# A per-slot list of weight-conversion steps for the first batch of a fused threshold-attention and GELU kernel

## The chip, the cores and the metric

The kernel runs on one core of a Trainium2 chip. The metric is the device time of one execution in microseconds (us). Three executions of the kernel before took 1337.2, 1337.45 and 1339.41 us; their median, 1337.45 us, is the time before. One further execution was recorded by the profiler and is the source of every profile line below.

## What is computed

```python
def _attn_ref(q, k, v, tau):                      # q, k, v: (8, 8, 576, 64) float32
    scores = (1 / np.sqrt(64)) * np.matmul(q, k.transpose(0, 1, 3, 2))
    thresh = np.max(scores, axis=-1, keepdims=True) - tau
    scores = np.where(scores >= thresh, scores, -1e9)
    attn = np.exp(scores - np.max(scores, axis=-1, keepdims=True))
    attn = attn / (np.sum(attn, axis=-1, keepdims=True) + 1e-09)
    return np.matmul(attn, v)
# heads joined: x is (4608, 512); w_in (512, 2048) and w_out (2048, 512) arrive as float64
h = x @ w_in
g = 0.5 * h * (1.0 + erf(h / sqrt(2)))
out = (g @ w_out).astype(np.float32)
```

So there are 64 heads of attention (8 batches of 8 heads), in which only scores close to the row's maximum count, and after it a two-layer network with an exact GELU over 4608 tokens. The change touches the way the two weight matrices become float32.

## The kernel before, in words

**Pairs and slots.** Two heads of one batch form a pair `p` (0 to 31, four per batch). The queries of a pair are worked on in five chunks `i`: four chunks of 128 queries for each of the two heads (two units of work), and a fifth chunk, `i == NC`, that holds the last 64 queries of both heads (one unit). One (pair, chunk) is a slot `n`. The loop at L1086 runs over the slots, and each engine is given its instructions in the order in which this loop writes them. The first batch is slots 0 to 19: slots 0 to 7 are chunks 0 and 1 of pairs 0, 1, 2, 3; then come chunks 2, 3, 4 of pair 0 (slots 8 to 10), of pair 1 (11 to 13), of pair 2 (14 to 16) and of pair 3 (17 to 19). Slots 10, 13, 16 and 19 have one unit, the others two.

**One slot of the first batch**, in program order:

- `scores` (L408): TensorE computes q·k into `sc`, of which two buffers exist in PSUM. A buffer comes free when `softmax_tail` of the slot before has read it.
- `softmax_head`: for each unit VectorE takes the row maximum `nmx` (L420), GpSimd the threshold `thr` (L423), and ScalarE the exponential `p` (L425). `add_low_bits` (L224) puts the outstanding additions of converted weights on GpSimd; the newest one is put ahead of the first `thr`.
- `turn_qk_early` (L324 to L341) in slots 0, 2 and 4: TensorE transposes q and k of the next pair, and ScalarE copies them out.
- `gelus` (L603): ScalarE copies finished pieces `hT` of the first layer out of PSUM.
- `weigh_v`, `weigh_half` and `divide_early` (L544, L568, L463; ScalarE copies at L554, L570, L465; GpSimd products at L471): the weighted values x^T of earlier chunks. In slots 12, 15 and 18 this is the long form, with 320 columns.
- `fill` (L636, L651): TensorE works on the two-layer network of finished tokens, from slot 10 on.
- `turn_p_early` (L354, ScalarE copies at L361, L365, L370, L374): transposes the exponentials of the slot before.
- `softmax_tail` (L441): VectorE sets exponentials below the threshold to zero and sums the rest.
- loads of later pairs: `load(HP)` in slot 13 and `load(HP + 1)` in slot 17 put 16 DMAs each on SP's queue.
- `convert` (L1160), the last large part of a slot.

TensorE's transposes, scores' partners `xT`, `tr`, and the network's `hT` share four PSUM buffers (tag "mm"), each freed by the copy that reads it.

**Conversion.** The weights come as 32 pieces of 128 x 512 float64 numbers, 512 KB each (16 of `w_in`, 16 of `w_out`). `load_piece` (L183) puts a load on SP's queue; eight are loaded at the start, and each finished piece starts the load of the next. A step of the generator `conversions` (L186) handles one piece: ScalarE makes a scaled copy of the high words (L202, `power`) and a copy of the low words (L203, into the weights), one piece ahead; VectorE shifts and masks (L210) and joins sign and magnitude (L211) in the older piece; GpSimd adds the two parts (L224) in the next slot. `fill` takes a matmul only when the pieces that it reads are converted.

**How many steps in which slot.** `convert(ns)` adds `ns` to a debt and takes steps until the debt is gone; each finished step pays 1060. Slot 0 adds nothing, slots 1 and 2 add 1200 each, later ones 1900, and slot 19 takes what is left. This gives two steps in most slots and one in some. `yield None` holds the last two pieces back for slot 19.

Of the kernel before, what the change touches and what calls it, by code (L numbers as in the profile page):

```python
# [18 lines left out]
def kernel(  # L19
# [141 lines left out]
    def load_piece(eng=nc.sync):  # L161
        k = loaded[0]
        if k == len(pieces):
            return
        staged = k % 2 and k < len(pieces) - LATER
        if wide and not staged and not x_free:
            return
        dst, src = pieces[k]
        loaded[0] += 1
        if not wide:  # L170
            nc.sync.dma_start(dst, src)
            converted[0] += 1
            load_piece()
            return
        slot = []
        if staged:

            half, at = divmod(k // 2 % 4, 2)
            raw = pd[half].bitcast(U32)[:, at * 2 * PIECE:(at + 1) * 2 * PIECE]
        else:  # L180
            slot = [x_slot()]
            raw = x_rows(slot[0]).bitcast(U32)
        eng.dma_start(raw, src.bitcast(U32))  # L183
        raws.append((dst, raw, slot))

    def conversions():  # L186

        vec = nc.vector
        ahead = []
        done = 0
        while raws or ahead:
            if raws:
                dst, raw, slot = raws.pop(0)
                lo, hi = (raw.rearrange("p (f w) -> p f w", w=2)[:, :, i] for i in range(2))  # L200
                power = gp.tile([P, PIECE], U32, tag="g", name="power")
                nc.scalar.activation(power.bitcast(FP32), hi.bitcast(FP32), AF.Copy, bias=0.0, scale=2.0 ** -112)  # L202
                nc.scalar.activation(dst.bitcast(U32), lo, AF.Copy, bias=0.0, scale=2.0 ** -29)  # L203
                ahead.append((dst, hi, power, slot))
                yield 0
            if len(ahead) == LATER and done == len(pieces) - LATER:
                yield None
            if len(ahead) == 2 or not raws:
                dst, hi, power, slot = ahead.pop(0)
                vec.tensor_scalar(power, power, 3, 0x7FFFFFF8, op0=ALU.logical_shift_left, op1=ALU.bitwise_and)  # L210
                vec.scalar_tensor_tensor(power, hi, 0x80000000, power, op0=ALU.bitwise_and, op1=ALU.bitwise_or)  # L211
                x_free.extend(slot)
                sums_due.append((dst.bitcast(U32), power))
                load_piece()
                done += 1
                yield 1060

    sums_due = []

    def add_low_bits(newest=False):  # L220

        for _ in range(min(1, len(sums_due)) if newest else len(sums_due)):
            dst, power = sums_due.pop(-1 if newest else 0)
            nc.gpsimd.tensor_tensor(dst, power, dst, op=ALU.add)  # L224
            converted[0] += 1
# [3 lines left out]
    def convert(ns, least=0):  # L229

        if conv["steps"] is None:
            conv["steps"] = conversions()
        conv["debt"] += ns
        while conv["debt"] > 0 or least > 0:
            took = next(conv["steps"], None)
            if took is None:
                return
            conv["debt"] -= took
            least -= took
# [5 lines left out]
    def load(p):  # L245
        for _ in load_steps(p):
            pass
# [151 lines left out]
    def scores(p, i):  # L399
        s = st[p]  # L400
        n = 1 if i == NC else 2
        sc = s["sc", i] = [ps.tile([P, 2, 512], FP32, tag="sc", name="sc", bufs=2) for _ in range(n)]
        for h in range(2):
            for e in range(n):
                rows = slice(0, P) if i == NC else slice(e * D, (e + 1) * D)
                lhsT = s["q_tail"] if i == NC else s["qT"][rows, i * P:(i + 1) * P]
                at = h * HALF + (TAIL if p < EARLY and e == 0 else 0)
                nc.tensor.matmul(  # L408
                    sc[e][:, h, 0:HALF], lhsT=lhsT, rhs=s["kT"][rows, at:at + HALF], start=True, stop=True)
# [37 lines left out]
    def invert(p, i):  # L447

        den = st[p]["sum", i]
        nc.vector.reciprocal(den, den)  # L450
# [608 lines left out]
    BATCH = HP * SLOTS  # L1059
# [16 lines left out]
    PARTS = 1.3, 1.3, 0.2, 1.3, 0.9  # L1076

    HALVED = (2, 3)
    BUSY = {1: 2, 6: 2, 8: 2, BATCH: 4}

    tokens = 0
# [4 lines left out]
    for n in range(len(slots) + WEIGH + 1):  # L1086
        p, i = slots[n] if n < len(slots) else divmod(n, SLOTS)
        early = p < EARLY
        last = slots[n - 1] if 0 < n <= len(slots) else None
        if p < NP:  # L1090
            scores(p, i)
            softmax_head(p, i)
            add_low_bits()
            if last and last[0] < EARLY:
                invert(*last)
            if p < HP - 1 and i == 0:
                turn_qk_early(p + 1)
        elif n == len(slots):
            early_end.close()
            weights_first()  # L1100
        gelus(0)
        if n == BATCH:
            gelus_held()
        table()
        for args in due:
            if len(args) == 2:
                weigh_half(*args)
                if args[1]:
                    divide_early(args[0], 0, TOK)
                continue  # L1110
            weigh_v(*args)
            divide_early(*args)
        due = []
        if p > EARLY and i == WEIGH:
            for lo, hi in (0, WIDE), (WIDE, S):
                weigh_v(p - 1, lo, hi)
            if p == NP:
                divide(p - 1)
        owed += (goal(n) - goal(n - 1)) * BLK_NS * (PARTS[i] if not early and p < NP else 1.0)
        if early:  # L1120
            fill(owed, tokens)
            owed = 0.0
            table()
        if last and last[0] < EARLY and last[1] < NC:
            turn_p_early(*last)
        if p < NP:
            softmax_tail(p, i)
        if p < NP and not early:
            turn_p(p, i)
        if p < NP and not early:  # L1130
            if i == 2:
                regroup(p, 1)
            if i > 2:
                regroup(p, i)
            if i == NC:
                divisors(p)
        if last and last[0] < EARLY and last[1] == NC:
            turn_p_early(*last)
        if p < 2 and i == 0:
            for _ in range(2):  # L1140
                load_piece()
            load_v_early(p + 2)
        if p == 1 and i == NC:
            load(HP)
        if n == BATCH - 3:
            load(HP + 1)
        if n == BATCH:
            for t in pd_tail + [turned_p[:, e, h, :, :] for e in range(2) for h in range(2)]:
                nc.gpsimd.memset(t[:, NB:4 * KR, :], 0.0)
        if EARLY < p < NP and i == DIVIDE:  # L1150
            divide(p - 1)
        if p >= HP and i == 1 and p + 2 < NP:
            loads = load_steps(p + 2)
        if p >= HP:
            next(loads, None)
        if p >= HP and i == 1 and p + 1 < NP or p == HP - 1 and i == 2:
            scale_q(p + 1)
        if p >= HP - 1 and i == 2 and p + 1 < NP:
            turn_qk(p + 1)
        convert(0 if n == 0 else 1200 if n < 3 else 1900 if n < BATCH - 1 else 1e9)  # L1160
        if not early:
            lag[0] = 2 if p < NP else 0
            if n != BATCH:
                share = 0.4 if n == BATCH + 1 else 1.0
                fill(owed * share, tokens)
                owed *= 1.0 - share
        if n in BUSY:
            keep_busy(BUSY[n])
        if last and last[0] < EARLY:
            if last[1] < 2 and last[0] in HALVED:  # L1170
                due.append((last[0], last[1]))
            elif last[1] == 1:
                due.append((last[0], 0, TOK))
            if last[1] == NC:
                due.append((last[0], TOK, S))
        if n == START - 1:
            tokens = TOK
        elif n == BATCH + 1:
            tokens = S
        elif p > EARLY and i == DIVIDE and p % HP == 0 or p == NP and i == WEIGH:  # L1180
            tokens = p // HP * S
            leaving += [n for n in AWAY if n in x_blk and (n + 1) * TOK <= tokens]
        elif leaving and i < 2:
            put_away(leaving.pop(0))
# [35 lines left out]
```

## Time and profile before

| | before |
|---|---|
| median of three executions | 1337.45 us |
| the profiled execution, its own time | 1338.74 us |
| span of its instructions on the core | 1336.9 us |
| TensorE busy in the span | 1318.9 us (99%) |
| VectorE, ScalarE, GpSimd busy | 1038.9, 605.4, 633.6 us |
| conversions: ScalarE L202, L203 | 32 + 32 instructions, first at 16.88 us, last at 124.05 us |
| conversions: VectorE L210, L211 | 32 + 32 instructions, first at 17.61 us, last at 128.19 us |
| conversions: GpSimd L224 | 32 instructions of 1270 ns |

The table mixes three kinds of number. The span runs from the first to the last instruction of the profiled execution; its own time is 1.84 us longer, for what lies around the instructions. Busy times are sums over the whole span, and say little of one stage: the first batch ends some 130 us after the start, and only there do conversions run. The profile can be asked for each engine's instructions in order of time, with the idle time before each and the engine that ended it; for the busy time of every engine in a stretch; and for the chain of work that ended last. Times in it count from the start of the span. The slots can be read off VectorE's row maxima (L420), whose first one in a slot marks it:

| slot | first row maximum, us | steps of conversion in the slot |
|---|---|---|
| 1 | 13.69 | 2 |
| 2 | 19.82 | 1 |
| 3 | 25.47 | 2 |
| 4 | 32.58 | 1 |
| 5 | 37.41 | 2 |
| 6 | 44.36 | 2 |
| 7 | 49.79 | 2 |
| 8 | 55.75 | 2 |
| 9 | 61.17 | 1 |
| 10 | 66.08 | 2 |
| 11 | 71.50 | 2 |
| 12 | 76.93 | 2 |
| 13 | 86.31 | 1 |
| 14 | 90.55 | 2 |
| 15 | 96.68 | 2 |
| 16 | 105.15 | 2 |
| 17 | 110.15 | 2 |
| 18 | 117.94 | 0 |
| 19 | 124.29 | 2 |
| 20 | 129.03 | |

The third column counts VectorE's pairs L210, L211 between one slot's `p` (L441) and the next slot's maximum.

### The profile page before, as it was taken

To read this page: it belongs to the slowest core of one execution; us is meant where nothing else is said; L and a number is where in the kernel's file an instruction comes from. 1 tells how busy PE (TensorE), PEld (TensorE's weight loads), DVE (VectorE), ACT (ScalarE), POOL (GpSimd) and SP (SyncE) were. 2 spreads that over 40 slices of the span, in tenths; PEclk is the share of its full clock that TensorE was granted. 3 is DMA by queue.
4 is the path that set the end of the run, shared out by engine and by line. 5 is a ranking of instruction groups with operands and counts; after the bars stand their busy time and mean duration, and the time that the engine had idled before them with its cause. 6 is when DMAs were issued, how large, how long until landed. Compare 5 with 4: busy or idle time off the path is not lost.

```text
span 1336.9 us, 19969 instructions
## 1 busy us (share of the span) xinstructions
PE 1318.9 (99%) x6362; PEld 893.4 (67%) x6362; DVE 1038.9 (78%) x2005; ACT 605.4 (45%) x1029; POOL 633.6 (47%) x1061
## 2 busy tenths in 40 slices
PE   8899999999999999999999999999999999999998
PEld 6677466466466466457556557568787787877877
DVE  6877777788888888888888888783857698386775
ACT  7987457268367358338438438322211113211120
POOL 3655454555555555545546551245264503635530
PEclk9999999999999999999999999999999999999999
DMA  8553566776776786786787775400000130000003
GB/s 258 196 150 62 124 151 141 167 183 153 175 188 153 179 201 153 180 209 155 165 219 164 164 187 124 106 9 1 1 0 1 40 101 18 0 1 0 1 0 79
DMA packets 209784, 152.42 MB, mean 114 GB/s; under 512 B 113360, under 2 KB 193088, under 8 KB 209680
## 3 DMA queue, kind: packets, MB, share of 16 engines
q1 hardware_dynamic: 192256, 127.21, 40.1%
q0 software_dynamic: 16992, 23.64, 6.7%
q8 instruction: 52, 0.85, 0.3%
q14 instruction: 52, 0.43, 0.1%
q10 hardware_dynamic: 432, 0.30, 0.1%
HBM read 55.97 MB, written 12.52 MB: 51 GB/s over the span
## 4 chain that ended last, share of the span: by engine, by line
PE 92%; DVE 2%; ACT 2%; DMA 2%; SPq 1%; issue 1%; POOL 0%; ACTq 0%; DVEq 0%
PE bank L824 34%; PE o_ps L651 17%; PE hT L636 16%; PE sc L408 13%; PE xT L544 11%; ACT p L425 1%; DVE nmx L420 1%; DMA q<-in_q_dram 1%; PE tr L354 1%; DMA x<-xall 1%; DVE power L211 1%; DMA turned_p<-in_moe_w_in_dram 0%; ACT pT L361 0%; DVE p L441 0%; DVE power L210 0%
## 5 line engine op out<-in xcount | busy, mean ns | idle before, releaser
L425 ACT ACTIVATE p<-sc,nmx 128x576 f32<-128x576 f32 x288 | 201.8, 737 | 272.7 <-DVE nmx L420 272.2
L441 DVE SCALAR_TENSOR_TENSOR p<-sc,thr,p 128x576 f32<-128x576 f32 x288 | 225.3, 816 | 74.8 <-ACT p L425 65.1
L423 POOL TENSOR_SCALAR thr<-nmx,tau_eff 128x1 f32<-128x1 f32 x288 | 83.9, 293 | 341.9 <-DVE nmx L420 337.6
L636 PE MATMUL hT<-xall,w_in 128*128 128x256 f32 x1024 | 242.0, 386 | 0.5 <-ACT g L603 0.5
L420 DVE TENSOR_REDUCE nmx<-sc 128x1 f32<-128x576 f32 x288 | 205.4, 750 | 44.5 <-PE sc L408 43.1
L651 PE MATMUL o_ps<-w_out,g 128*128 128x512 f32 x512 | 236.8, 603 | 0.0
L636 PEld LDWEIGHTS hT<-xall,w_in 128*128 128x128 f32 x1024 | 189.3, 190 | 50.8 <-issue 23.0
L706 DVE TENSOR_TENSOR c<-c,bank 128x320 f32<-128x320 f32 x304 | 146.7, 487 | 34.2 <-PE bank L824 21.0
L706 DVE TENSOR_TENSOR o<-o,bank 128x256 f32<-128x256 f32 x240 | 99.8, 419 | 93.7 <-PE bank L824 88.7
L651 PEld LDWEIGHTS o_ps<-w_out,g 128*128 128x128 f32 x512 | 93.1, 190 | 109.2 <-issue 106.8
L408 PE MATMUL sc<-kT,qT 64*128 64x288 f32 x960 | 159.9, 431 | 2.1 <-DVE p L441 1.6
L544 PE MATMUL xT<-pT,v 128*64 128x320 f32 (+1 forms) x1240 | 159.9, 411 | 0.6 <-DVE pT L365 0.5
L505 DVE STREAM_TRANSPOSE turned_p<-p 128x1152 f32<-128x1152 f32 x112 | 154.4, 1378 | 3.9
L408 PEld LDWEIGHTS sc<-kT,qT 64*128 64x128 f32 x960 | 91.0, 186 | 75.8 <-issue 60.1
L544 PEld LDWEIGHTS xT<-pT,v 128*64 128x64 f32 x1240 | 86.7, 137 | 71.9 <-issue 11.3
L824 PE MATMUL bank<-w_out,c 128*128 128x256 f32 x480 | 120.2, 381 | 0.5 <-DVE o L706 0.5
L267 POOL DMA_DIRECT2D v<-in_v_dram x208 | 110.8, 536 | 4.3 <-issue 2.1
L824 PEld LDWEIGHTS bank<-w_out,c 128*128 128x128 f32 x480 | 89.9, 190 | 18.8 <-DVE o L706 3.0
L877 ACT ACTIVATE c<-c 128x320 f32<-128x320 f32 (+1 forms) x80 | 46.9, 623 | 114.6 <-DVE c L706 114.5
L824 PE MATMUL bank<-t_out,c 128*128 128x256 f32 x320 | 82.8, 381 | 0.0
L706 POOL TENSOR_TENSOR c<-c,g 128x320 f32<-128x320 f32 (+1 forms) x40 | 50.5, 1271 | 67.5 <-DVE c L706 67.5
L824 PE MATMUL bank<-t_out,g 128*128 128x256 f32 x320 | 82.1, 379 | 0.0
(180 smaller groups left out, 1757.7 us busy)
## 6 DMA issues: line engine op xcount, KB each, us to landing
pT<-turned_p SPq DMA_DIRECT2D x448, 160.0 KB, 3.5
pT<-pd_tail SPq DMA_DIRECT2D x112, 80.0 KB, 2.7
q<-in_q_dram POOLq DMA_DIRECT2D x104, 72.0 KB, 3.7
k<-in_k_dram POOLq DMA_DIRECT2D x104, 72.0 KB, 3.1
inv<-turned SPq DMA_DIRECT2D x54, 128.0 KB, 4.0
v<-in_v_dram POOLq DMA_DIRECT2D x156, 40.0 KB, 3.1
out_dram<-o SPq DMA_DIRECT2D x40, 128.0 KB, 2.3
xall<-in_moe_w_out_dram SPq DMA_DIRECT2D x9, 512.0 KB, 4.1
```

The costliest lines, as they stand in the source:

```text
L267: eng.dma_start(t[r:P:4, e, 0:n, :], rows[:, r * KR:r * KR + n, :])
L408: nc.tensor.matmul(sc[e][:, h, 0:HALF], lhsT=lhsT, rhs=s["kT"][rows, at:at + HALF], start=True, stop=True)
L420: nc.vector.tensor_reduce(nmx[:, e:e + 1], sc, axis=AXIS.XY, op=ALU.max, negate=True)
L423: nc.gpsimd.tensor_scalar(thr[:, e:e + 1], nmx[:, e:e + 1], -1.0, tau_eff, op0=ALU.mult, op1=ALU.subtract)
L425: nc.scalar.activation(w[:, e * S:(e + 1) * S].rearrange("p (h s) -> p h s", h=2), sc, AF.Exp, bias=nmx[:, e:e + 1], scale=1.0)
L441: nc.vector.scalar_tensor_tensor(row, sc[e][:, :, 0:HALF], thr[:, e:e + 1], row, op0=ALU.is_ge, op1=ALU.mult, accum_out=den[e])
L505: nc.vector.transpose(turned_p[:, :, i // 2, 0:NB, i % 2 * Q:(i % 2 + 1) * Q], w.rearrange("p (e b i) -> p e b i", e=2, i=Q))
L544: nc.tensor.matmul(to, lhsT=s["v"][:, e, c, :], rhs=rhs, start=(c == 0), stop=(c == KR - 1))
L636: nc.tensor.matmul(hT[:, j % 2, :], lhsT=w_in_sb[c][:, j * P:(j + 1) * P], rhs=x_blk[n][:, c, :], start=(c == 0), stop=(c == N_DM - 1))
L651: nc.tensor.matmul(o[:, 0:d_model], lhsT=g[j][:, m * P:(m + 1) * P], rhs=w_out_sb[j], start=(j == 0), stop=(j == N_DF - 1))
L706: eng.tensor_tensor(out, a, b, op=ALU.add)
L824: nc.tensor.matmul(to, lhsT=l, rhs=r, start=start and k == 0, stop=k == len(pairs) - 1, skip_group_check=not start)
```

## The change

The debt in nanoseconds gives way to a list `STEPS` with the number of steps for each slot from 0 to 18. A finished step now counts 1, and `convert(0, STEPS[n])` takes steps until that number is reached, or until `yield None`. Slot 19 takes the rest, as before.

```diff
@@ conversions @@
-                yield 1060
+                yield 1
...
     HALVED = (2, 3)
+    STEPS = [0, 1, 1, 1, 1, 1, 2, 1, 2, 1, 2, 2, 3, 2, 2, 3, 2, 2, 3]
...
-        convert(0 if n == 0 else 1200 if n < 3 else 1900 if n < BATCH - 1 else 1e9)
+        if n < BATCH - 1:
+            convert(0, STEPS[n])
+        else:
+            convert(1e9)
```

The built program differs from the one before in this: VectorE has one pair L210, L211 less in slots 1, 3, 5 and 7, and one more in slots 12, 13, 15 and 18. ScalarE's pairs L202, L203 follow one piece ahead of these (slot 1 has two pieces on ScalarE where it had three, slot 18 has two where it had one). TensorE's order is the same, instruction for instruction. On SP's queue six loads of pieces stand behind the 16 loads of `load(HP)`, where three stood; on GpSimd's the additions follow their pieces. The number of instructions of each kind is the same.

## The prediction

> **What bounds the kernel now.** I first read the page's totals, then the busy time of each engine in stretches of 10 us, then each engine's instructions in order of time.
>
> ```profile
> PE 1318.9 (99%) x6362; PEld 893.4 (67%) x6362; DVE 1038.9 (78%) x2005; ACT 605.4 (45%) x1029; POOL 633.6 (47%) x1061
> ```
> ```profile
> 40.00:50.00 10.00, 8.67 (x90) 6.77 (x87) 9.23 (x20) 9.64 (x20) 4.40 (x7) 1.00 0.35 116
> 90.00:100.00 10.00, 10.00 (x70) 7.22 (x67) 8.46 (x20) 8.83 (x19) 5.29 (x9) 1.00 0.64 110
> ```
>
> Over the span TensorE (PE) is busy 99%, so time can only be won where it waits. The stretches (columns: length, then PE, PEld, VectorE, ScalarE, GpSimd, clock, DMA share, GB/s) show where: from 40 to 50 us TensorE is busy 8.67 us and ScalarE 9.64; from 90 to 100 us TensorE is full. So slots 1 to 9 hang on ScalarE and VectorE, slots 13 to 16 on TensorE. ScalarE in slot 7:
>
> ```profile
> 50.57 1.41 ACT L425 ACTIVATE p<-sc,nmx 128x576 f32<-128x576 f32 x2 [0.42 <-DVE nmx L420]
> ...
> 54.53 0.73 ACT L202 ACTIVATE power<-xall 128x512 f32<-128x512 f32 x1
> 55.12 0.72 ACT L203 ACTIVATE w_in<-xall 128x512 uint32<-128x512 uint32 x1
> 56.53 1.41 ACT L425 ACTIVATE p<-sc,nmx 128x576 f32<-128x576 f32 x2 [0.69 <-DVE nmx L420]
> ```
>
> It works without a gap up to the end of the second piece, then waits 0.69 us for the next row maximum. That maximum stands on VectorE behind the second conversion:
>
> ```profile
> 53.08 0.96 DVE L210 TENSOR_SCALAR power<-power 128x512 uint32<-128x512 uint32 x1
> 54.08 0.69 DVE L211 SCALAR_TENSOR_TENSOR power<-xall,power 128x512 uint32<-128x512 uint32 x1
> 54.69 0.42 DVE L210 TENSOR_SCALAR power<-power 128x512 uint32<-128x512 uint32 x1
> 55.14 0.69 DVE L211 SCALAR_TENSOR_TENSOR power<-turned_p,power 128x512 uint32<-128x512 uint32 x1
> 55.75 1.42 DVE L420 TENSOR_REDUCE nmx<-sc 128x1 f32<-128x576 f32 x2
> ```
>
> The scores of slot 8 were due from TensorE at about 54.4 us, so one conversion would fit into that wait and the second doesn't. Slot 12, ScalarE, then TensorE:
>
> ```profile
> 83.37 1.07 ACT L361 COPY pT<-tr 128x512 f32<-128x512 f32 x2 [3.06 <-PE tr L354]
> ...
> 85.69 0.66 ACT L202 ACTIVATE power<-turned_p 128x512 f32<-128x512 f32 x1
> 86.25 0.67 ACT L203 ACTIVATE w_out<-turned_p 128x512 uint32<-128x512 uint32 x1
> 87.10 0.74 ACT L425 ACTIVATE p<-sc,nmx 128x576 f32<-128x576 f32 x1 [0.17 <-DVE nmx L420]
> 87.73 0.58 ACT L603 COPY g<-hT 128x512 f32<-128x512 f32 x1
> ```
> ```profile
> 87.74 1.60 PE L354 MATMUL tr<-ident,p 128*128 128x128 f32 x9
> ```
>
> ScalarE idles 3.06 us here, but ahead of the pT copy, which waits for TensorE; the conversions stand behind that copy. And TensorE's nine transposes take 1.60 us (elsewhere 1.15): five of them begin at 88.37, just after the copy of hT frees a PSUM buffer at 88.31. So ScalarE's lateness here is at once TensorE's.
>
> **What the Trainium skill says.** "TensorE: Matmul & The Clock Gate", section "What's actually happening": the clock falls to half after an idle window of about 3.4 us. The trace agrees:
>
> ```profile
> 21.00:22.00 1.00, 0.10 (x1) 0.00 (x0) 0.66 (x3) 1.00 (x3) 1.00 (x4) 1.00 0.53 149
> 24.00:25.00 1.00, 1.00 (x7) 0.48 (x4) 0.27 (x1) 0.98 (x3) 0.58 (x1) 0.50 0.91 299
> ```
>
> After a gap from 21.1 to 22.64 us the clock is 0.50 from about 23.6 to 27 us. The same page, "Architectural detail", says that ScalarE and VectorE run strictly in order; the two slots above show it. "SBUF — State Buffer", section "SBUF: two separate sides": VectorE and GpSimd share a port pair, and the later one waits. The L210 of 0.96 us above (median 0.424) stands beside a GpSimd L471 at 53.03 to 53.76.
>
> **The change, part by part.** Prices: a piece on ScalarE takes 1.15 us (two steps of 0.57 from start to start); a pair on VectorE 1.07 us (53.08 to 54.69 is 1.6 with the port wait, 54.69 to 55.75 is 1.06).
>
> *Removed in slots 1, 3, 5, 7* (interval from one exponential to the next, before; after).
> - Slot 1: 14.48 to 20.60, 6.12 us. VectorE's one pair ends 18.7, the maximum follows, exponential at 19.45: saves 1.15.
> - Slots 2 and 3: slot 2 is full on ScalarE (5.87 us), so it moves as a whole, and slot 3's exponential to 25.3. But TensorE's transposes of q and k don't move, so the gap that ended at 22.64 shrinks from 1.53 to about 0.4 us, and I expect no half clock. Then slot 3's scores take 1.24 us for 2.08, xT 2.5 for 3.18, and xT, from the copy of pT it needs (24.1), ends at 26.6 for 28.5. ScalarE's copies of xT, inv and pT are done 2.3 us after that, as now (28.5 to 30.79), and one piece later, at 30.0, comes the exponential of slot 4, now at 33.37: 3.35 in all, so 2.2 more than slot 1 gave (1.37 if the half clock stays: a piece and the wait of 0.2 behind it).
> - Slot 5: 5.91 us, full on ScalarE. Without a piece 4.5; VectorE's one pair (0.4 port wait) gives 4.65: saves 1.25.
> - Slot 7: 5.96. One pair with its port wait ends 1.1 sooner, and a little from GpSimd: saves 1.2.
>
> Sum: 5.8 us by slot 9; bounds 4 (half clock stays, scores late) and 6.5. Slots 4, 6, 8, 9 keep their counts and lengths.
>
> *Added in slots 12, 13, 15, 18.* In slot 12 ScalarE's third piece comes after 86.84, VectorE's third pair waits for it, GpSimd's newest addition (1.27) precedes the threshold: the exponential of slot 13 moves from 87.10 to 88.2, the copy of hT, the transposes and the scores of slot 14 with it: +1.1. Slot 13, in today's times with 1.1 added: VectorE's first pair ends at 91.1; the second waits for ScalarE's copies of pT and the L202 of its piece (91.5) and ends at 92.6; the maximum follows, and the exponential of slot 14 stands at 93.4 for 91.34, 2.0 late: +0.9. Slot 15's scores begin at 93.78, the masks of slot 14 end at 93.67, so there is no slack. In slot 15 ScalarE waits for TensorE at the copy of pT anyway (2.17 us idle), but then three pieces follow where two did; slot 17's scores wait for slot 16's mask (ended 107.71): +1.1. In slot 18 VectorE's pair lies in its 2.97 us idle time, free; with that cover gone it would cost 1.07. ScalarE's second piece pushes slot 19's exponential by 0.7, of which 0.5 reaches slot 20's maximum. Sum +3.6; bounds 1.5 (slots 12 and 15 hidden) and 4.5.
>
> *Queues.* SP: the 16 loads of slot 13 take 10.6 us to issue (86.84 to 97.46), and six pieces, not three, come behind them: in the changed kernel from about 81.5 + 10.6 = 92 us. At the 110 to 186 GB/s moved between 90 and 110 us a piece of 512 KB lands every 2.8 to 4.8 us (an estimate). The first two are on ScalarE at about 105, the next two at 112: hidden, with 1 to 8 us spare. GpSimd: a third addition follows the thresholds of slots 13 and 16 and delays only a product for tokens used later: nothing, and at most 1.27 us each if that product were awaited.
>
> Net: -5.8 + 3.6 = -2.2 us. From slot 20 on both kernels are the same and TensorE is full, so the shift stays. Span 1336.9 - 2.2 = 1334.7; with the 1.84 us around it 1336.5 against 1338.74. That execution lay 1.3 above the median, so the median goes from 1337.45 to 1335.2.
>
> **Rivals.**
> 1. The late steps hide in the idle time before the long x^T's copies (3.06 and 2.17 us). For it: ScalarE and VectorE are idle there. Against: the order in the queues. Then only slots 13 and 18 cost, 1.5: net -4.3, 1333.2.
> 2. The early slots win less, since TensorE or the half clock binds at once: -4 + 3.8 = -0.2, 1337.2. For it: TensorE is busy 87% there. Against: its gaps (1.33 us in slots 6 and 8) all end on ScalarE.
> 3. Slower: pieces come late behind `load(HP)` on SP. ScalarE then waits in slot 16 or 17, with exponentials queued behind it, and TensorE follows. Against: 1 to 8 us of margin by the estimate above. It decides once the landing is more than 5 us past the need (2.2 lost again and 2.7 more); at 6 us late, 1341.2.
> 4. That the steps don't move is excluded by the built order.
>
> **How the numbers follow.** 0.2% is 2.67 us, about what a measurement of this kernel can tell from no change; faster means below 1334.8. Forecast (-1.2 to -3.4): 0.50, of which 0.15 lies below the bound. Rival 1: 0.26, nearly all faster (0.25). Rival 2: 0.16, no change. Rival 3: 0.08. Faster 0.15 + 0.25 = 0.40, slower 0.08, the rest, 0.52, within. The range leaves out rival 3 and the edges: 1332.6 to 1337.8.
>
> **What would show it.** Right: row maxima of slot 4 near 29 us and slot 10 near 60.2 (66.08 before), clock 1.00 from 23 to 27 us; slot 17 near 107 (110.15 before), slot 20 near 126.8 (129.03). Slot 13 less slot 12 should grow from 9.38 to about 10.5 us. Wrong: an exponential at slot 13 no later after the copy of pT than now (rival 1), a half clock elsewhere (2), or ScalarE's L202 waiting for a DMA (3).

## The result, and the profile after

| | before | changed |
|---|---|---|
| median (executions) | 1337.38 us (10) | 1340.75 us (10) |
| lowest to highest | 1335.36 to 1339.41 | 1337.22 to 1342.93 |
| the profiled execution, its own time | 1338.74 | 1337.22 |
| its span | 1336.9 | 1335.4 |
| its mean TensorE clock | 0.998 | 0.999 |

The changed kernel takes 1.0027 times as long (95% interval 1.0017 to 1.0038), 3.4 us more. The forecast was 1335.2 us, 2.2 us less than before. The mean TensorE clock is the clock that TensorE was granted, as a share of full speed, averaged over the execution.

The profiled execution of the changed kernel is the fastest of its ten; the other nine took 1339.75 to 1342.93 us at mean clocks of 0.995 to 0.998. So its profile shows where work stands and what waits, but not the whole of the loss. In it slot 0 also began 0.92 us sooner than in the profile of before, so the slots are compared below from slot 0.

The total of TensorE, from the page of the changed kernel:

```profile
PE 1317.2 (99%) x6362; PEld 892.3 (67%) x6362; DVE 1041.2 (78%) x2005; ACT 604.9 (45%) x1029; POOL 635.5 (48%) x1061
```

The share did not move. Busy time by stretch does show the change (columns as in the prediction; the clock is the third from the right):

```profile
21.00:22.00 1.00, 1.00 (x10) 0.72 (x9) 0.97 (x4) 0.94 (x5) 0.34 (x1) 1.00 0.33 86
24.00:25.00 1.00, 1.00 (x12) 0.67 (x10) 0.09 (x2) 1.00 (x2) 0.29 (x1) 1.00 0.87 250
...
40.00:50.00 10.00, 9.72 (x93) 7.21 (x92) 9.42 (x21) 8.97 (x20) 5.91 (x11) 1.00 0.49 154
80.00:90.00 10.00, 7.45 (x41) 5.43 (x40) 8.60 (x17) 8.56 (x18) 8.38 (x10) 1.00 0.79 173
90.00:100.00 10.00, 9.98 (x68) 7.49 (x68) 6.49 (x13) 6.79 (x16) 5.20 (x8) 1.00 0.72 239
```

From 40 to 50 us TensorE rose from 8.67 to 9.72 us, and at 21 and 24 us it is full at full clock: the gap of 1.53 us and its half clock are gone. But from 80 to 90 us it is busy only 7.45 us (9.68 before). Idle time has moved from the early slots to the late ones.

ScalarE, then VectorE, in slot 7 of the changed kernel (start, length, instruction; in square brackets the idle time before it and what ended it):

```profile
47.66 0.73 ACT L202 ACTIVATE power<-xall 128x512 f32<-128x512 f32 x1
48.23 0.73 ACT L203 ACTIVATE w_in<-xall 128x512 uint32<-128x512 uint32 x1
49.73 1.40 ACT L425 ACTIVATE p<-sc,nmx 128x576 f32<-128x576 f32 x2 [0.78 <-DVE nmx L420]
```
```profile
47.34 0.96 DVE L210 TENSOR_SCALAR power<-power 128x512 uint32<-128x512 uint32 x1
48.34 0.69 DVE L211 SCALAR_TENSOR_TENSOR power<-turned_p,power 128x512 uint32<-128x512 uint32 x1
48.95 1.42 DVE L420 TENSOR_REDUCE nmx<-sc 128x1 f32<-128x576 f32 x2
```

One conversion instead of two stands ahead of the row maximum, and the exponential of the next slot comes 4.90 us after that of slot 7 where it came 5.96 us after it. ScalarE in slots 12 and 13, then every gap of TensorE of over 0.5 us in slots 13 to 17:

```profile
76.53 1.07 ACT L361 COPY pT<-tr 128x512 f32<-128x512 f32 x2 [3.06 <-PE tr L354]
...
81.41 0.74 ACT L425 ACTIVATE p<-sc,nmx 128x576 f32<-128x576 f32 x1 [0.18 <-DVE nmx L420]
82.04 0.58 ACT L603 COPY g<-hT 128x512 f32<-128x512 f32 x1
...
87.37 1.40 ACT L425 ACTIVATE p<-sc,nmx 128x576 f32<-128x576 f32 x2 [0.97 <-DVE nmx L420]
```
```profile
82.67 0.81 PE L354 MATMUL tr<-ident,p 128*128 128x128 f32 x5 [1.17 <-ACT g L603]
...
89.37 1.94 PE L408 MATMUL sc<-pd_tail,qT 64*128 64x288 f32 x8 [1.38 <-DVE p L441]
...
104.56 0.33 PE L354 MATMUL tr<-ident,p 128*128 128x128 f32 x1 [1.21 <-ACT pT L361]
...
111.18 0.33 PE L354 MATMUL tr<-ident,p 128*128 128x128 f32 x1 [1.10 <-ACT g L603]
```

The pT copy still waits 3.06 us, and the exponential now starts 4.88 us after it begins, where it was 3.73: the third piece is not hidden. TensorE's transposes, one run of 1.60 us before, now break in two with a gap of 1.17 us. In the profile of the kernel before, no gap of TensorE between 78 and 125 us is over 0.45 us. Four of over 1 us are new.

The slots from one first row maximum to the next, in us:

| slots | before | changed | difference | forecast |
|---|---|---|---|---|
| 1 | 6.13 | 4.99 | -1.14 | -1.15 |
| 2 and 3 | 12.76 | 10.52 | -2.24 | -2.2 |
| 5 | 6.95 | 5.69 | -1.26 | -1.25 |
| 7 | 5.96 | 4.90 | -1.06 | -1.2 |
| the others up to slot 9 | | | -0.24 | 0 |
| **0 to 9** | 56.54 | 50.60 | **-5.94** | -5.8 |
| 12 | 9.38 | 10.53 | +1.15 | +1.1 |
| 13 | 4.24 | 5.97 | +1.73 | +0.9 |
| 14 and 15 | 14.60 | 15.91 | +1.31 | +1.1 |
| 16 and 17 | 12.79 | 13.70 | +0.91 | 0 |
| 18 and 19 | 11.09 | 11.52 | +0.43 | +0.5 |
| **12 to 19** | 52.10 | 57.63 | **+5.53** | +3.6 |

The early gain is what was forecast. Slots 13 and 16 lose some 0.9 us each that was not, and nine executions lost more still.

### The profile page after: what moved, and what is told of

Its sections match the earlier page's. It is cut to its first block, busy times and chain, and to the rows that moved or that the text cites. A ratio compares the mean times of both kernels' runs of the same rounds, so it can differ in the third digit from the quotient of the medians.

```text
span 1335.4 us, 19968 instructions
## 1 busy us (share of the span) xinstructions
PE 1317.2 (99%) x6362; PEld 892.3 (67%) x6362; DVE 1041.2 (78%) x2005; ACT 604.9 (45%) x1029; POOL 635.5 (48%) x1061
## 4 chain that ended last, share of the span: by engine, by line
PE 90%; DVE 3%; ACT 3%; DMA 1%; issue 1%; SPq 1%; POOL 0%; DVEq 0%; ACTq 0%; POOLq 0%
PE bank L824 34%; PE o_ps L651 16%; PE hT L636 16%; PE sc L408 12%; PE xT L544 11%; DVE nmx L420 1%; ACT p L425 1%; DVE power L211 1%; DVE p L441 1%; DVE power L210 1%; DMA x<-xall 0%; ACT pT L361 0%; PE tr L354 0%; DMA q<-in_q_dram 0%; PE tr L463 0%
## 5 line engine op out<-in xcount | busy, mean ns | idle before, releaser
L441 DVE SCALAR_TENSOR_TENSOR p<-sc,thr,p 128x576 f32<-128x576 f32 x288 | 225.3, 816 | 75.6 <-ACT p L425 66.1
```

What stands on the lines that cost most here:

```text
L441: nc.vector.scalar_tensor_tensor(row, sc[e][:, :, 0:HALF], thr[:, e:e + 1], row, op0=ALU.is_ge, op1=ALU.mult, accum_out=den[e])
```

## The experiments

Two things had to be explained: 1.9 us in slots 13 and 16 of the profile, and why most executions are some 3 us longer than that profile. My theory for the first: in slots 13 and 16 a third addition of GpSimd blocks VectorE. For the second: the new gaps of TensorE bring back the half clock. The rivals: a third conversion simply costs more than I priced, through ScalarE's queue and the gaps as such; or the difference is chance or the chip.

### The changed kernel again, on other chips

No edit. 

> The changed kernel once more, to see its spread. Theory A (the clock): TensorE's new gaps in slots 13 to 17 let the clock fall to half in most executions, in windows whose phase differs from run to run; then time and mean clock go together, 1.34 us for each 0.001 of mean clock (0.1% of 1340 us): executions at 0.999 near 1337, at 0.996 near 1341, and the kernel before lies at 0.998 to 0.999. Theory B (plain waits): the third conversion steps simply hold up TensorE in every execution; then the times scatter by 1 us or less at one clock. The change should come out 3 us slower than before under A, by whatever the windows give; under B the same as its profiled execution, no slower than before.

The first repeat gave 1338.47 us (13 executions) against 1337.48: 1.0011 (1.0002 to 1.0021), 1.0 us more, where 3 had been expected if the clock was the cause. Three of the 13 took 1340.72 to 1343.53 at clocks of 0.995 to 0.997; the rest took 1337.8 to 1339.2, two of them at 0.997 as well. So the long executions are at low clocks, but the mean clock does not fix the time of each one. To catch the low clock in a profile, three more repeats were made on two other chips.

> The changed kernel once more, for a profile of an execution at a lower mean clock. Theory A: such a profile shows the same slots up to 12, and a stretch of about 3.4 us (or several) at half clock that begins in or just after one of TensorE's gaps at 81.5, 88, 103.4 or 110 us; each such stretch makes the execution 1 to 2 us longer than one at 0.999. If the profile is again at 0.999, it shows 10.5, 6.0, 5.5, 10.4, 6.0 us for slots 12 to 16, as twice before.

> As the look before it: the changed kernel, for another profile. Theory A expects about every second execution at 0.997 or less with half clock between 81 and 115 us.

> The changed kernel, on the same chip, as the measure for the two runs beside it: 1338.5 to 1341.5, with a third or more of its executions at 0.997 of the clock or below.

In this order they gave 1341.64 (12), 1340.57 (8) and 1340.6 us (21), ratios 1.0030 (1.0021 to 1.0038), 1.0019 (1.0005 to 1.0033) and 1.0018 (1.001 to 1.0025). All three profiles show two stretches of half clock in the late slots: one behind a late gap (of 1.21 us in slot 16 in the first of them, of 1.38 us in slot 14 in the other two) and one around slot 21. Busy time by stretch in the second of them, an execution of 1341.67 us:

```profile
88.00:90.00 2.00, 0.62 (x6) 0.41 (x4) 1.67 (x5) 2.00 (x5) 2.00 (x4) 1.00 0.69 111
90.00:92.00 2.00, 1.98 (x8) 1.14 (x8) 1.93 (x6) 1.94 (x7) 0.75 (x2) 0.76 0.24 54
92.00:94.00 2.00, 2.00 (x8) 0.77 (x8) 2.00 (x4) 1.78 (x4) 1.17 (x1) 0.50 0.26 62
...
136.00:138.00 2.00, 2.00 (x10) 0.95 (x8) 1.28 (x2) 2.00 (x5) 0.58 (x2) 0.50 0.00 0
```

TensorE's instructions there, in that execution and then in the first profile of the same kernel:

```profile
89.92 2.65 PE L408 MATMUL sc<-pd_tail,qT 64*128 64x288 f32 x8 [1.38 <-DVE p L441]
92.50 3.85 PE L544 MATMUL xT<-pT,v 128*64 128x320 f32 x20
```
```profile
91.24 2.91 PE L544 MATMUL xT<-pT,v 128*64 128x320 f32 x20
```

The gap before the scores is 1.38 us in both. In one execution the clock stays at 1.00, in the other it is 0.50 from about 91 to 94.5 us, and the scores take 2.65 us for 1.94, x^T 3.85 for 2.91. Slot 15 lasts 12.09 us for 10.44. The half clock from about 135.4 to 138.8 us makes slot 21 last 9.50 for 7.81. Together 3.3 us. A busy TensorE at half clock looks full in the busy column; only the clock column and the length of known groups tell.

What follows: the longer executions hold half clock that the first profile did not. The Trainium skill, "TensorE: Matmul & The Clock Gate", section "What's actually happening", says that the window is free-running, so that the turning point depends on where in it the work lands; that would fit one gap with two outcomes, though no run here can set the phase. The three profiles fit it too: each stretch of half clock lasts 3.41 or 3.42 us, and the two of one profile begin 27.3, 44.4 and 44.4 us apart, which is 8, 13 and 13 times 3.41. The same section speaks of an idle window of about 3.4 us. Here the measurement decides otherwise: 1.38 us idle within a stretch of 3.4 us that was otherwise busy was enough.

The length of a gap alone does not decide. In the kernel before, gaps of nearly that length in slots 4, 6 and 8 (1.24, 1.33 and 1.33 us) were followed by no half clock in either of its two profiles. The first two of them:

```profile
35.40 0.80 PE L354 MATMUL tr<-ident,p 128*128 128x128 f32 x5 [1.24 <-ACT qT L327]
...
46.77 1.16 PE L304 MATMUL idle<-ident 128*128 128x128 f32 x8 [1.33 <-ACT xall L570]
```

The half clock around slot 21 follows two short gaps, 0.75 us before its scores and 0.52 us before its x^T. In the execution of 1341.67 us:

```profile
132.68 1.94 PE L408 MATMUL sc<-kT,qT 64*128 64x288 f32 x8 [0.75 <-DVE p L441]
```

What else counts, no run here tells.

### The additions deferred

```diff
-    def add_low_bits(newest=False):
+    def add_low_bits(newest=False, keep=0):
...
-        for _ in range(min(1, len(sums_due)) if newest else len(sums_due)):
+        for _ in range(min(1, len(sums_due)) if newest else max(0, len(sums_due) - keep)):
...
-            add_low_bits()
+            add_low_bits(keep=1 if n in (13, 14, 16, 17) else 0)
```

> As the changed kernel, but the second addition that GpSimd has left over in slots 13 and 16 waits until slots 15 and 18. Theory A: VectorE's L211 of 1.65 us in slots 13 and 16 waits for that addition (0.96 us longer than usual, twice); without it these are 0.7 to 1.1 us, the shift from slot 12 to slot 20 falls from 5.5 to about 3.6 us, TensorE's gaps there shrink by about 1 us each, and so does the half clock: 1336 to 1338, at 0.997 to 0.999. If the port has no part in it: as the changed kernel, 1340.7.

1336.4 us (13), 0.9993 (0.9985 to 1.0001) of before, and 2.07 us under the repeat of the changed kernel on the same chip. VectorE in slot 13 and, in the last line, in slot 16 of the changed kernel, then GpSimd in slot 13:

```profile
83.95 1.65 DVE L211 SCALAR_TENSOR_TENSOR power<-xall,power 128x512 uint32<-128x512 uint32 x1
...
86.59 1.42 DVE L420 TENSOR_REDUCE nmx<-sc 128x1 f32<-128x576 f32 x2
...
105.83 1.66 DVE L211 SCALAR_TENSOR_TENSOR power<-turned_p,power 128x512 uint32<-128x512 uint32 x1
```
```profile
82.36 1.28 POOL L224 TENSOR_TENSOR w_in<-power,w_in 128x512 uint32<-128x512 uint32 x1
83.58 1.47 POOL L224 TENSOR_TENSOR w_out<-power,w_out 128x512 uint32<-128x512 uint32 x1
```

and on VectorE with the addition deferred:

```profile
84.12 0.69 DVE L211 SCALAR_TENSOR_TENSOR power<-xall,power 128x512 uint32<-128x512 uint32 x1
...
85.97 1.42 DVE L420 TENSOR_REDUCE nmx<-sc 128x1 f32<-128x576 f32 x2
```

L211 reads two operands from SBUF. It stands beside GpSimd's addition from 83.58 to 85.05 and ends at 85.6, 0.96 us later than its length alone gives; the row maximum behind it moves with it. Without the addition, slot 13 lasts 5.18 us for 5.97, slot 16 5.01 for 5.97, and slots 12 to 19 take 3.85 us more than before where it was 5.53, close to the 3.6 forecast. The gaps of 1.17 and 1.21 us in slots 13 and 16 are still there, at full clock in this profile; that of slot 14 is down to 0.60, and slot 17 has none over 0.5.

### The port wait alone, in the kernel before

```diff
-    def add_low_bits(newest=False):
+    def add_low_bits(newest=False, twice=False):
...
+            if twice:
+                nc.gpsimd.tensor_tensor(power, power, power, op=ALU.add)
...
-            add_low_bits()
+            add_low_bits(twice=n in (13, 16))
```

It adds one GpSimd instruction of 1.10 us in slots 13 and 16 to the kernel before, over a buffer that is no longer needed.

> The kernel before, with one thing added: in slots 13 and 16 GpSimd does one more addition of 1.27 us (over a buffer that is no longer needed), where the changed kernel has its third. It prices the port alone, at the old places of the conversions. If VectorE's L211 waits for GpSimd there: 1.4 to 1.7 us for 0.69 in slots 13 and 16, the maxima of slots 14 and 17 0.7 and 1.0 us later, about 1.5 us on the whole (1339), and 1.0 to 1.9 us more where the longer gap brings a half clock. If the third addition costs nothing, as the prediction had it: 1337.4.

1339.11 us (21) against 1337.94: 1.0010 (1.0003 to 1.0016), 1.17 us more. VectorE's and GpSimd's instructions in slot 13 of it:

```profile
89.95 1.41 DVE L211 SCALAR_TENSOR_TENSOR power<-turned_p,power 128x512 uint32<-128x512 uint32 x1
```
```profile
89.71 1.10 POOL L226 TENSOR_TENSOR power<-power 128x512 uint32<-128x512 uint32 x1
```

L211 takes 1.41 us in both slots for 0.69, and slot 17 comes 1.67 us later, counted from slot 0. So one more GpSimd instruction that nobody awaits does cost time, and the conversions on ScalarE and VectorE are not needed for it. Taken away in one run and added in the other, the instruction beside L211 is shown to be the cause; that the wait is for a shared port is what the Trainium skill says, cited below.

### TensorE kept busy in the late gaps

Repeated transposes, whose results are the same, in the places of the gaps. First trial:

```diff
+    AGAIN = {(1, 3, 0): 2, (2, 3, 1): 2, (2, 4, 0): 2}
...
-            for c in range(NC):
-                turn(tr[:, c, :], e * (S + TAIL) + c * P)
+            for _ in range(1 + AGAIN.get((p, i, e), 0)):
+                for c in range(NC):
+                    turn(tr[:, c, :], e * (S + TAIL) + c * P)
...
-    BUSY = {1: 2, 6: 2, 8: 2, BATCH: 4}
+    BUSY = {1: 2, 6: 2, 8: 2, 14: 2, BATCH: 4}
```

> As the changed kernel, but TensorE does idle work in its four gaps: the transposes ahead of the gaps in slots 13, 16 and 17 are done three times over, and slot 14 has 8 idle matmuls. The results are the same. Theory A (the clock): no half clock in the first batch, mean clock 0.999 in all executions, and the time falls from 1340.7 to about 1336 to 1337.5, the scatter with it. Theory B (plain waits): nothing gained, 1340 to 1342, or a little slower for the added matmuls.

1338.81 us (13), 1.0008 (1.0 to 1.0017): not lower than the changed kernel beside it. TensorE in slot 14:

```profile
89.70 1.16 PE L304 MATMUL idle<-ident 128*128 128x128 f32 x8 [1.32 <-ACT g L606]
```

The idle matmuls of slot 14 themselves waited for a PSUM buffer and came behind the gap, where they added 1.16 us. On this chip long executions were also rare in the changed kernel. Twelve of the 13 ran at a clock of 0.999 or 1.0, yet the time did not fall to the 1336 to 1337.5 that was expected. With work added in the path, the trial decides nothing. The second leaves the idle matmuls out and puts repeats into slot 14's transposes:

```diff
+    AGAIN = {(1, 3, 0): 2, (1, 4, 0): 2, (2, 3, 1): 2, (2, 4, 0): 2}
```

> The changed kernel with TensorE's four gaps filled by repeated transposes alone (slots 13, 14, 16, 17); the earlier fill put idle matmuls in slot 14, which waited for a buffer themselves and came after the gap. The results are the same. Theory A (the half clock makes most of the loss): on a chip where the changed kernel itself stands at 1340 or more, this one stands at 1337 to 1338.5, with mean clocks of 0.998 to 1.000. If the half clock only goes along with something else: as the changed kernel, whatever the clock.

1338.39 us (13), 1.0004 (0.9996 to 1.0012), against 1340.6 (21), 1.0018 (1.001 to 1.0025), for the changed kernel on the same chip: 2.2 us less, though it does more. All 13 ran at a mean clock of 0.999 or 1.0, where 13 of the 21 had been at 0.997 or less. TensorE in slots 13 and 14:

```profile
82.94 0.82 PE L356 MATMUL tr<-ident,p 128*128 128x128 f32 x5 [0.30 <-ACT g L606]
...
89.65 1.95 PE L411 MATMUL sc<-pd_tail,qT 64*128 64x288 f32 x8 [0.52 <-DVE p L444]
```

The scores of slot 14 start no earlier than in the changed kernel (89.65 against 89.37), so the gaps themselves cost nothing more than the wait they stand for; what went is the half clock. It went around slot 21 too, where the gaps of 0.76 and 0.52 us stand unfilled in this profile; why is not known.

### Both removed

```diff
+    AGAIN = {(1, 3, 0): 2, (1, 4, 0): 1, (2, 3, 1): 2}
...
+            add_low_bits(keep=1 if n in (13, 14, 16, 17) else 0)
```

> The changed kernel without both suspects: GpSimd's third additions deferred, and the gaps that are left in slots 13, 14 and 16 filled with repeated transposes. Theory A: port 1.9 us and half clock both gone: 1335 to 1336 with mean clocks of 0.999 to 1.000, about 2 us below the run with filled gaps alone, which is what the prediction had (1335.2). If one of the two is no cause, it stands no lower than the better of the runs with one suspect removed.

1336.92 us (13), 0.9995 (0.9987 to 1.0004): 3.7 us under the changed kernel on the same chip, where one cause removed gave 2.1 and 2.2. It is still above the 1335 to 1336 that was expected, and 1.5 us, not 2, below the run with filled gaps. Its profile still has half clock from about 132.3 to 135.7 us, where the repeats do not reach. Five of the executions ran at a mean clock of 1.000; they took 1334.44 to 1337.3 us, median 1335.1.

### The half clock of the early slots alone

The kernel before, with repeats in slot 2 only: `AGAIN = {(0, 1, 0): 2}`, and the loop over it as above.

> The kernel before, with one thing added: in slot 2 TensorE makes the four transposes of slot 1's first unit three times over, which fills 0.9 us of the 1.53 us gap at 21.1 us; the results are the same. It prices the half clock of slots 2 and 3, which the changed kernel avoids. If the half clock is worth what it seems, all executions run at 0.999 to 1.000 of the clock and at about 1335.3, where the fastest of the kernel before lie, 2 us below its median; then 2 of the 5.9 us that the changed kernel wins by slot 10 are no merit of moved conversions. If the half clock is hidden behind ScalarE, the time stays at 1337.4.

1336.05 us (21) against 1337.94 (50): 0.9987 (0.9981 to 0.9994), 1.9 us less. TensorE in slot 2, and busy time by stretch:

```profile
23.07 0.81 PE L356 MATMUL tr<-ident,p 128*128 128x128 f32 x5 [0.67 <-ACT qT L327]
```
```profile
24.00:25.00 1.00, 1.00 (x8) 0.49 (x6) 0.69 (x1) 0.96 (x4) 0.21 (x2) 1.00 0.81 209
```

With a gap of 0.67 us for 1.53 the clock stays at 1.00. So a part of the early gain of the changed kernel can be had without moving a conversion. How large a part is less clear than the median: from slot 0 to slot 10 this profile takes 55.57 us where the one of before takes 56.54, 0.97 less, and the difference stays 0.94 up to slot 22. The rest of the 1.9 us is not seen in the slots.

> The kernel before against itself: 1337.4, ratio 1.000 within 0.1%. It shows the spread of the comparison and a second profile; where that profile has no half clock in slots 2 and 3, slot 10 begins about 1 to 2 us sooner than in the first one (66.08 less 9.54 for slot 0).

The kernel before against itself, with no edit, gave 1337.84 (13), 1.0000 (0.9992 to 1.0008): differences of some 0.1% are this measurement's noise. Its profile has the half clock of slots 2 and 3 too.

### Other lists

Four lists for `STEPS`, of which the first is that of the change:

```diff
-    STEPS = [0, 1, 1, 1, 1, 1, 2, 1, 2, 1, 2, 2, 3, 2, 2, 3, 2, 2, 3]
+    STEPS = [0, 1, 1, 1, 1, 1, 2, 1, 2, 1, 2, 2, 2, 2, 2, 2, 2, 2, 4]
```

> The early cuts stay (slots 1, 3, 5, 7), but no slot up to 17 has three steps: slots 12 and 15 have two as before, slot 13 two, and slot 18 three with VectorE (four pieces on ScalarE). Theory A: the two largest gaps (1.2 us each in slots 13 and 16) and the port waits go, slot 13 still costs 0.9, slot 18 costs about 2 for four pieces on ScalarE: net -5.9 + 2.9 = -3 us, 1334 to 1336 at 0.998 to 0.999. If the early cuts themselves bring the loss: 1340 or more.

1337.54 us (13), 1.0000 (0.9991 to 1.0008); missed. Slots 13 and 16 last 5.18 and 5.00 us, with no port wait, and no gap of TensorE from slot 12 to slot 18 is over 0.5 us. But with the four steps of slot 18 comes one of 2.59 us, which ends at 124.67 us, and half clock from about 124.1 to 131.1 us.

```diff
+    STEPS = [0, 1, 1, 1, 1, 1, 2, 1, 2, 1, 2, 2, 2, 1, 2, 2, 2, 2, 2]
```

> As the run with the last two pieces in slot 20, but slot 13 keeps its one step and slot 19 has two. Slot 13's second step cost 1.1 us by slot 17 in the runs without threes; in slot 19 a piece more stands on ScalarE, where the slot had 0.8 us to spare. If slot 13's place is the dearer one: 1332.5 to 1333.5. If slot 19's piece delays slot 20's exponential, and the GELUs behind it, by its full 1.15 us: 1333.6 to 1334.5.

1337.79 us (12), 1.0006 (0.9997 to 1.0015); missed too. In slot 19 three pieces stand on ScalarE ahead of slot 20's exponential, the third waits 0.97 us for an addition of GpSimd, and VectorE's mask (L441), which frees the buffer for slot 21's scores, waits 2.00 us for the exponential. TensorE there:

```profile
128.56 3.00 PE L408 MATMUL sc<-kT,qT 64*128 64x288 f32 x8 [2.99 <-DVE p L441]
131.49 4.88 PE L544 MATMUL xT<-pT,v 128*64 128x320 f32 x20
```

Again a gap, 2.99 us, and half clock: eight scores of 3.00 us (1.94 at full clock).

```diff
+    STEPS = [0, 1, 1, 1, 1, 1, 2, 1, 2, 1, 2, 2, 2, 2, 2, 2, 2, 2, 2]
```

> The early cuts stay, no slot has three steps, slots 10 to 18 have two each, slot 19 one, and the last two pieces are finished on VectorE in slot 20, where the second layer's work covers them. Against the run without threes it takes two pieces off slot 18 on ScalarE. If the late costs are those of slots 13 to 16 as measured there (+1.1 by slot 17) and slots 18 to 20 cost 1.5 or less: 1334 to 1335.5, below both kernels. If slot 20's maximum of slot 21 is on the path, 2 us more: 1336 to 1337.5.

1333.64 us (6), 0.9969 (0.9957 to 0.9981): below both kernels and below the 1334 to 1335.5 that was expected, all six at a clock of 0.999. TensorE at slot 21's scores:

```profile
127.17 1.94 PE L408 MATMUL sc<-kT,qT 64*128 64x288 f32 x8 [0.80 <-DVE p L441]
```

That is the longest gap of TensorE between 78 and 140 us. No slot has three steps, so no third addition meets L211 in slots 13 and 16 (5.18 and 5.02 us), and the last two pieces end on VectorE in slot 20. It is the version to take, with the reserve that only six executions on one chip stand behind it.

## Why the prediction was wrong

- **Early slots, forecast -5.8 us: right**, -5.94; the slots that it names lie within 0.15 of their terms, the others together at -0.24. The half clock of slots 2 and 3 went as forecast. Row maxima: slot 4 at 28.28 us (near 29 was forecast), slot 10 at 59.22 (60.2; slot 0 itself began 0.92 earlier). The signs for the late slots failed: slot 17 at 108.47 (107 was forecast) and slot 20 at 127.72 (126.8).
- **Late slots, forecast +3.6: right for what it counted.** With the additions deferred, slots 12 to 19 take 3.85 us more. Slot 12 +1.15, slots 14 and 15 +1.31, slots 18 and 19 +0.43 lie within 0.25 of their terms in the changed kernel. Slots 13 and 16 were out, by the next step: without the third additions slot 13 is +0.94 (+0.9 was forecast) and slots 16 and 17 are level with before.
- **"Queues", the third addition of GpSimd: failed.** It "delays only a product for tokens used later: nothing". I looked only at who waits for GpSimd's result. What L211 needs meanwhile was left out: the Trainium skill, "SBUF — State Buffer", section "SBUF: two separate sides", which I had cited, names also a VectorE operation with two SBUF inputs against a GpSimd operation that reads SBUF, and says that the later one blocks. The trace agrees: L211 took 1.65 us for 0.69 in slot 13 and 1.66 in slot 16. The term was 0; it measured 5.53 - 3.85 = 1.7 us in the profile and 2.07 in the median where the addition was taken away, and 1.67 and 1.17 where an instruction was added to the kernel before.
- **The sum held no half clock in the late slots: failed.** I took out the half clock that leaves with slot 2's gap, and priced the late waits by their length alone. My own lines of slot 2 show half clock behind a gap of 1.53 us, less than half of the 3.4 us that I had cited beside them; so gaps of 1.1 to 1.4 us had to be feared as well. The gaps of the changed kernel (1.17, 1.38, 1.21, 1.10 us, and 0.78 before slot 21's scores, where 0.15 stood) go with half clock in most executions on two chips. The term was 0; two stretches cost 3.3 us in one profile, and filling the gaps gave 2.2 in the median. My list of signs did name "a half clock elsewhere", under rival 2, but at the price of losing the early gain, not as a term of its own.
- **"From slot 20 on ... the shift stays": failed** in the executions with half clock around slot 21. In the first profile what was left of it held in part: slot 20 stands 0.39 us and slot 22 0.19 us ahead of before, counted from slot 0.
- **From a profile to the median.** I took the 1.3 us by which one profiled execution lay above its median for the changed kernel too. Its own profiled execution lies 3.5 us below its median. That step had no ground.
- **Rivals.** The late steps did not hide (rival 1). The early slots did not win less (rival 2). Late landings (rival 3) did not occur: no L202 of ScalarE waited for a DMA. The slower case came by a mechanism that none of them held.

The sum, mended: -2.2 + 1.7 (port) + 3.3 (half clock of one profile) = +2.8 us, against +3.4 measured in the medians. The profiles bear it out. From slot 0's first row maximum to that of slot 22 the kernel before takes 133.08 us, the changed kernel 132.89 without half clock and 136.17 and 136.25 with two stretches of it (+3.1), the one with filled gaps 132.94, the one with deferred additions 131.17. By the medians of the experiments (2.07 and 2.2) the sum is only +2.1, so 1.3 us is open there, and more if the two overlap: deferring the additions also shrinks the gap of slot 14. With both causes removed the median falls by 3.7 us, not by the 5.6 between forecast and result. That its executions at full clock lie at 1335.1, the number of the forecast, is in part luck: it picks the best, and the kernel before has 1335.55 and 1335.99 in its two executions at that clock beside it.

**What stays open.** Why the low clock makes most executions long on two chips and only 3 of 13 on another, and which gaps bring it. The half clock around slot 21 was not removed by itself. And executions at equal clock still differ by 1 to 2 us: the second trial of filled gaps lies at 1338.39 without half clock, which the port wait (2.07) brings down to 1336.3, not to 1335.2. A part of this lies outside the change: from slot 22 to the end, where all the kernels do the same work, the 16 profiles take between 1192.3 and 1195.2 us. The cause of that spread was not looked for.

## What to carry to other kernels

An instruction moved onto an idle engine is not free because nobody waits for its result: ask also whether it reads SBUF on GpSimd while VectorE runs an instruction with two SBUF operands. A wait that moves from one stage to another can take the half clock with it, so list TensorE's gaps after the change, short ones that stand close together too, and price a possible half clock behind each. A single profile can be one of the fortunate executions: compare its time and clock with those of the others before its trace is read as the kernel.

## What was not expected of the hardware

- A TensorE gap of 1.38 us was followed by half clock in one execution and not in another, for the same kernel. Gaps of 1.24 and 1.33 us in the kernel before were not followed by it, while two of 0.75 to 0.80 and 0.52 us close together were in four of the ten profiles that have them.
- Half clock over some 3.4 us costs 1 to 2 us: 1.65 in slot 15 and 1.69 in slot 21 of one profile; for slots 2 and 3, 0.97 in the profile and 1.9 in the median.
- Where L211 met GpSimd's addition both grew: L211 from 0.69 to 1.65 us, the addition from 1.27 to 1.47.
